# Linear attention and a two-layer MLP in one kernel: the whole hand-written order of steps is replaced

## The chip, the cores and the metric

The kernel runs on one core of a Trainium2 chip. The metric is the device time of one execution in microseconds (us); lower is better. TensorE (PE) multiplies matrices, VectorE (DVE), ScalarE (ACT) and GpSimd (POOL) do elementwise work, SyncE (SP) issues most transfers. Each engine takes its instructions strictly in the order in which the program lists them.

## The reference

A linear attention with a decayed state, for 4 batches, 8 heads, 768 positions and head size 48, whose output goes through a two-layer MLP with a smooth ReLU:

```python
for t in range(S):                       # r, k, v: (B, H, S, D) = (4, 8, 768, 48); w, u: (H, D)
    cur = einsum('bhd,bhe->bhde', u[None] * kt, vt)
    y[:, :, t] = einsum('bhd,bhde->bhe', rt, state + cur)
    state = w[None, :, :, None] * state + einsum('bhd,bhe->bhde', kt, vt)
x = y.transpose(0, 2, 1, 3).reshape(3072, 384)
h = x @ w_in                             # 384 x 2048
g = where(h >= 1, h, where(h <= -1, 0, (h + 1) ** 2 / 4))
out = g @ w_out                          # 2048 x 384
```

## The kernel before

**Tiling.** The 768 positions are cut into 6 chunks of 128, and the 4 batches into 2 pairs. A *group* g (0 to 11) is one chunk of one pair: g // 2 is the chunk, g % 2 the pair. A *unit* n (0 to 23) is one batch of a group: n = 2g + j. Groups 0 and 1 are the first chunk of the two pairs.

**Attention steps of a unit or group.** `load.K`, `load.R`, `loadV` fetch K, R and V (float32, runs of 48 numbers; in groups 0 and 1 in halves by unit, `load.K.0.1` being the second half of group 0). `Ks` and `Rs` scale K and R by powers of the decay (tables made by `Wdn_p`, `Wup_p`, `Wdn`, `Wup` from `bcw`'s product `wb`); `KU` is K times u (`bcu`, `u_bc`), `RKU` is R times KU, `usum` sums it over a head into `diag`, `V` casts V to bfloat16, `V2` is V times diag (a tile that the listings print as `V_` with a number). `T` transposes Ks and Rs on PE for groups 0 to 2 and `TT` copies them out; from group 3 on `KRT` does it by a DMA transpose. `A` multiplies K by R; `AT` masks it into bfloat16, either on DVE in one instruction, or by an ACT copy (`AT.n.1`) and a POOL select (`AT.n.0`). `Sp` multiplies Ks by V, `Tm` adds it to the state (in groups 0 and 1 it writes the first state), `decay` scales the state, `sbf` casts it. `Y` multiplies AT by V and R by the state; `y` adds V2. `X` and `xT` turn y for the MLP: through PE for groups 0 to 2, by one DMA transpose on SP for groups from 3 on (tile `yy`, step `xT.8` for group 4).

**MLP steps.** `mm1.g.q.j` multiplies w_in's quarter q (512 of 2048 columns) by group g's xT into two PSUM banks `h0` to `h2` (j = -1: both units; 0 or 1: one unit, in group 0's first two quarters); `relu` and `square` on ACT and `gate` on DVE apply the smooth ReLU; `mm2.g.j.q` adds quarter q's share to unit j's output; `o` copies it out of PSUM and `out` stores it. Weights are fetched by POOL with a cast to bfloat16: `w_in.0` and `w_in.1` bring quarters 0, 1 and 2, 3; `w_out.q` brings quarter q:

```python
    def w_in_go(e, bk, i):
        n = slice(i * DF // W_IN, (i + 1) * DF // W_IN)
        nc.gpsimd.dma_start(out=w_in_sb[:, :, n], in_=w_in_src[:, :, n])
    def w_out_go(e, bk, i):
        n = slice(i * nF // W_OUT, (i + 1) * nF // W_OUT)
        nc.gpsimd.dma_start(out=w_out_sb[:, n, :], in_=w_out_src[:, n, :])
```

**What sets the order.** A text table, `ORDER`, names every step once; a loop at the end of the kernel runs them in that order, so the table fixes the order on every engine. In a token such as `V.1.0@A:1`, `@A` names the engine (A, D or P), the digits behind the colon the buffers or PSUM banks, and `~5` puts five *idle products* (products of zeros) ahead of the step on PE; `warm.18` is 18 idle products by themselves. Waits follow from the data and the buffers.

```python
    for token in ORDER.split():
        token, _, idles = token.partition("~")
        idle[0] = int(idles or 0)
        name, _, bufs = token.partition(":")
        name, _, e = name.partition("@")
        kind, *args = name.split(".")
        if kind == "warm":
            keep_warm(int(args[0]), *args[1:])
        elif kind in do:
            do[kind](e, [int(x, 36) for x in bufs], *[int(x) if x.lstrip("-").isdigit() else x for x in args])
```

Lines that the profile names: L526 `mm1`, L554 `mm2`, L544 `gate`, L534 `relu`, L539 `square`, L406 `A`, L421, L412 and L416 `AT`, L446 and L441 `Y`, L432 `Sp`, L388 `T`, L501 `X`, L327 `Ks` and `Rs`, L337 `KU`, L344 `RKU`, L355 and L357 `usum`, L369 and L367 `V2`, L468 `y`, L476 and L484 `Tm`, L489 `decay`, L290 `w_in`, L294 `w_out`, L304 the loads, L398 `KRT`, L511 `xT` by DMA, L587 `out`, L204 and L608 idle products, L237 `bcw`, L242 `bcu`, L257 the tables, L232 `lw`. L212 is the helper that copies and casts, for `V`, `TT`, `sbf`, `xT`, `o` and `u_bc`.

Of the kernel before, what the change touches and what calls it, by code (L numbers as in the profile page):

```python
# [14 lines left out]
P = 128  # L15
# [25 lines left out]
usum.1.0@A:1 A.1:0~8 V2.0.0@P:0 Ks.2.0@P:2 AT.2.0:1 loadV.2.0:0 V2.1.0@A:1 Y.0:1 T.3:2 sbf.0@A Tm.2@D usum.0.1@D Y.2:0
TT.3@D:3 y.2:0 AT.1.1:2 Rs.2.0@P:2 A.3:1~14 X.2:0 V2.0.1@A y.0:1 AT.3.0:3 warm.2.h.2 X.0:1 T.5:2~8 AT.1.0 xT.2@A:0
T.4:0 TT.5@D:0 Y.1:0 w_in.1 load.K.3.0:0 xT.0@A:1 sbf.1@A usum.1.1@D A.5:1 mm1.0.0.0:2 KU.2.0@P:0 y.1:2 TT.4@D:1
load.R.3.0:0 V.1.1@A X.1:1 Y.3:0 AT.5.0:0 A.4:0 V2.1.1@P xT.1@A mm1.0.0.1 V.2.0@A:2 Sp.5:1 y.3:0 RKU.2.0@P:0
relu.0.0:0 X.3:0 Tm.5@D:0 mm1.0.1.0:1 AT.4.0:1 xT.3@A decay.5 square.0.0:0 usum.2.0@D:0 Sp.4:1 mm1.0.1.1 w_out.0 Y.4:0
relu.0.1:1 mm1.1.1.-1:0 gate.0.0:0 square.0.1:1 Tm.4@D:1 mm1.0.2.-1:2 relu.1.1:0 Y.5:1 square.1.1:0 V2.2.0@P:0 w_out.1
y.4:1 gate.0.1:1 w_out.2 X.4:0 w_out.3 mm1.0.3.-1:1 xT.4@A:2 gate.1.1:2 relu.0.2:1 Sp.3:0 y.5:2 mm1.1.0.-1:0
square.0.2:1 Tm.3@D KU.3.0@P:1 decay.4 gate.0.2:3 relu.0.3:0 relu.1.0:1 mm2.0.0.0:1 mm2.0.1.0:0 Ks.3.0@P:0
square.1.0:0 KRT.K.3:0 mm1.1.3.-1:2 mm2.0.1.1 Rs.3.0@P:0 RKU.3.0@P:1 mm2.0.0.1 square.0.3:1 gate.1.0:4 mm2.0.1.2 gate.0.3:5
relu.1.3:1 loadV.3.0:1 mm2.0.0.2 mm1.1.2.-1:0 square.1.3:0 usum.3.0@D:1 mm2.0.0.3 relu.1.2:0 KRT.R.3:0 mm2.0.1.3  # L50
o.0.0@D:0 square.1.2:1 mm2.1.0.0:1 o.0.1@D gate.1.3:6 load.K.4.0:1 X.5:0 mm2.1.0.1 load.R.4.0:1 xT.5@A V.3.0@A:3
mm1.2.3.-1:1 gate.1.2:7 sbf.3@A V2.3.0@P:1 Sp.7:0 A.7:2 loadV.4.0:0 relu.2.3:1 Tm.7@D:0 A.6:0 mm2.1.0.2 AT.6.0:2
sbf.2@A square.2.3:0 Ks.4.0@P:2 sbf.4@A Sp.6:0 mm2.1.0.3 load.K.5.0:2 Tm.6@D:1 mm1.2.0.-1:0 o.1.0@A:1 AT.7.0:3 decay.6
Y.6:0 Y.7:1 relu.2.0:0 KRT.K.4:1 y.6:0 mm1.2.1.-1:2 KU.4.0@P:0 y.7 V.4.0@A:4 gate.2.3:8 xT.6:1 RKU.4.0@P:0
square.2.0:1 mm2.1.1.0:0 Sp.8:1 mm2.1.1.1 load.R.5.0:2 Tm.8@D:1 relu.2.1:1 load.K.6.0:0 mm1.2.2.-1:1 gate.2.0:9
Ks.5.0@P:1 mm2.1.1.2 square.2.1:0 mm2.2.0.0:1 mm2.1.1.3 decay.7 Rs.4.0@P:1 mm1.3.0.-1:0 gate.2.1:0 relu.2.2:0
square.2.2:1 KRT.K.5:0 mm2.2.0.1 o.1.1@D sbf.5@A relu.3.0:1 mm1.3.1.-1:2 gate.2.2:1 out.1 KU.5.0@P:1 square.3.0:0
Rs.5.0@P:2 mm2.2.0.2 relu.3.1:0 gate.3.0:3 mm1.3.2.-1:1 KRT.R.4:1 square.3.1:1 loadV.5.0:1 load.R.6.0:0 usum.4.0@D:0
mm2.2.0.3 mm2.2.1.0:0 KU.6.0@P:0 relu.3.2:1 gate.3.1:5 mm1.3.3.-1:0 square.3.2:0 loadV.6.0:0 gate.3.2:4 mm2.2.1.1
V2.4.0@P:0 sbf.6@A o.2.0@A:1 A.9:2 sbf.7@A relu.3.3:0 A.8:1 AT.9.0:1 mm2.2.1.2 KRT.R.5:0 square.3.3:1 mm2.3.0.0:1  # L60
AT.8.0:0 out.0 decay.8 mm2.2.1.3 load.K.7.0:1 mm2.3.0.1 o.2.1@A gate.3.3:2 V.6.0@A:0 V.5.0@A:2 Y.8:0 Ks.6.0@P:0
mm2.3.0.2 y.8:1 Y.9:0 mm2.3.0.3 y.9 RKU.5.0@P:1 A.11:2 xT.8:0 o.3.0@A:0 A.10:1 usum.5.0@D:1 AT.11.0:2 mm2.3.1.0:0
Sp.10:1 KRT.K.6:1 mm2.3.1.1 Rs.6.0@P:0 RKU.6.0@P:0 Tm.10@D:0 mm2.3.1.2 load.R.7.0:1 Sp.9:1 mm2.3.1.3 Tm.9@D:1
V2.5.0@P:1 mm1.4.0.-1:0 AT.10.0:3 o.3.1@A sbf.8@A decay.9 decay.10 KRT.R.6:1 usum.6.0@D:0 relu.4.0:1 Sp.11:1 Y.10:0
mm1.4.1.-1:2 square.4.0:0 Tm.11@D:1 y.10:0 V2.6.0@P:0 Ks.7.0@P:2 Y.11:1 mm1.4.2.-1:1 loadV.7.0:0 out.2 relu.4.1:0
gate.4.0:7 y.11 A.12:0 xT.10:2 square.4.1:1 AT.12.0:0 mm2.4.0.0:0 Sp.12:1 relu.4.2:1 KU.7.0@P:1 square.4.2:0
gate.4.1:6 load.K.8.0:2 mm1.4.3.-1:0 V.7.0@A:1 KRT.K.7:0 gate.4.2:9 load.R.8.0:2 A.13:2 Rs.7.0@P:1 mm2.4.0.1 out.3
# [582 lines left out]
```

## Time and profile before

| what | us |
|---|---|
| median of 3 runs | 175.96 |
| the 3 runs | 175.46, 175.96, 178.86 |
| span of the profiled execution, first to last instruction | 176.4 |
| PE, ACT, DVE, POOL busy | 165.0, 135.2, 130.3, 120.2 |
| matmuls of the first layer (L526) / second layer (L554) | 72.0 / 71.9 |
| first product with w_in starts at | 22.05 |
| last elementwise instruction (L602) starts at | 172.93 |

No time but the span is kept of the profiled execution; the three runs are others. The page lists the busy time of each engine, the span in 40 slices of 4.4 us, the DMA queues, the chain of work that ended last and the costliest groups of instructions. In a row of the timeline the first number is the start, the second the length, then engine, line, operation, output<-inputs, and in brackets how long the engine was idle before and what released it. "DMA to landing" is the time from a transfer's issue to the arrival of its data.

### The profile page before, as it was taken

To read this page: it belongs to the slowest core of one execution; us is meant where nothing else is said; L and a number is where in the kernel's file an instruction comes from. 1 tells how busy PE (TensorE), PEld (TensorE's weight loads), DVE (VectorE), ACT (ScalarE), POOL (GpSimd) and SP (SyncE) were. 2 spreads that over 40 slices of the span, in tenths; PEclk is the share of its full clock that TensorE was granted. 3 is DMA by queue.
4 is the path that set the end of the run, shared out by engine and by line. 5 is a ranking of instruction groups with operands and counts; after the bars stand their busy time and mean duration, and the time that the engine had idled before them with its cause. 6 is when DMAs were issued, how large, how long until landed. Compare 5 with 4: busy or idle time off the path is not lost.

```text
span 176.4 us, 4159 instructions
## 1 busy us (share of the span) xinstructions
PE 165.0 (94%) x1684; PEld 125.2 (71%) x1684; DVE 130.3 (74%) x167; ACT 135.2 (77%) x194; POOL 120.2 (68%) x97
## 2 busy tenths in 40 slices
PE   6998699999999999779999999999999999999992
PEld 5776587766787766458686777885878767777671
DVE  5599779857987578727978889788895877461471
ACT  4399879996987995319989697989399994888540
POOL 6699999990899999999399799999349400000000
PEclk9999999999999999969999999999999999999998
DMA  5999999999999999996999997989982400312022
GB/s 109 221 219 192 216 175 234 207 165 209 238 172 196 191 202 252 158 183 175 196 221 211 185 183 159 266 149 243 194 197 93 89 17 4 97 37 89 4 89 89
DMA packets 106967, 28.78 MB, mean 163 GB/s; under 512 B 100930, under 2 KB 106180, under 8 KB 106948
## 3 DMA queue, kind: packets, MB, share of 16 engines
q1 hardware_dynamic: 103888, 25.24, 73.6%
q0 software_dynamic: 2912, 3.15, 11.4%
q8 instruction: 13, 0.21, 0.5%
q10 hardware_dynamic: 148, 0.13, 0.2%
q14 instruction: 6, 0.05, 0.1%
HBM read 20.45 MB, written 4.72 MB: 143 GB/s over the span
## 4 chain that ended last, share of the span: by engine, by line
PE 71%; DMA 13%; DVE 7%; ACT 5%; POOL 1%; issue 1%; DVEq 0%; POOLq 0%
PE hp L526 31%; PE op L554 30%; DMA VF<-in_v_dram 5%; DMA w_out_sb<-in_moe_w_out_dram 4%; DMA xT<-yy 3%; DVE AT L421 3%; PE A L406 2%; PE Y L446 2%; PE Y L441 2%; PE Sp L432 1%; ACT V L212 1%; PE ub L242 1%; POOL V L369 1%; PE wb L237 1%; ACT RKU L355 1%; DVE yy L468 1%
## 5 line engine op out<-in xcount | busy, mean ns | idle before, releaser
L526 PE MATMUL hp<-xT,w_in_sb 128*128 128x256 bf16 (+1 forms) x600 | 72.0, 271 | 3.4 <-DMA xT<-yy 2.2
L554 PE MATMUL op<-w_out_sb,gt 128*128 128x384 bf16 (+2 forms) x400 | 71.9, 320 | 0.1
L544 DVE SCALAR_TENSOR_TENSOR gt<-sq,hp 128x1024 bf16<-128x1024 f32 x48 | 57.9, 1216 | 16.2 <-ACT sq L539 16.1
L526 PEld LDWEIGHTS <-w_in_sb 128*128 128x128 bf16 x600 | 56.2, 99 | 13.9 <-issue 3.1
L534 ACT ACTIVATE pt<-hp 128x1024 f32<-128x1024 f32 x48 | 48.7, 1018 | 17.7 <-PE hp L526 17.4
L539 ACT ACTIVATE sq<-pt 128x1024 f32<-128x1024 f32 x48 | 50.4, 1057 | 1.2
L554 PEld LDWEIGHTS <-gt 128*128 128x128 bf16 x400 | 36.5, 98 | 19.3 <-issue 0.5
L421 DVE TENSOR_TENSOR AT<-A,umask 128x1024 bf16<-128x1024 f32 x22 | 26.5, 1218 | 2.2 <-PE A L406 1.9
L337 POOL TENSOR_TENSOR KU<-K,u_bc 128x768 f32<-128x768 f32 (+1 forms) x13 | 21.6, 1658 | 2.0 <-DVE u_bc L212 2.0
L344 POOL TENSOR_TENSOR RKU<-R,KU 128x768 f32<-128x768 f32 (+1 forms) x14 | 22.2, 1589 | 0.3
L489 POOL TENSOR_TENSOR state<-Tm,wCm 128x384 f32<-128x384 f32 x16 | 16.0, 1003 | 8.8 <-DVE Tm L476 8.6
L369 POOL TENSOR_TENSOR V<-V,diag 128x768 f32<-128x768 bf16 (+1 forms) x12 | 16.4, 1365 | 7.1 <-ACT V L212 4.7
L327 POOL TENSOR_TENSOR Ks<-Wdn,K 128x768 bf16<-128x768 f32 x10 | 18.2, 1818 | 1.2 <-DMA K<-in_k_dram 1.2
L327 POOL TENSOR_TENSOR Rs<-Wup,R 128x768 bf16<-128x768 f32 x10 | 18.2, 1819 | 0.1
L476 DVE TENSOR_TENSOR Tm<-Sp,state 128x384 f32<-128x384 f32 x16 | 8.9, 555 | 7.3 <-POOL Ks L327 3.4
L468 DVE TENSOR_TENSOR yy<-Y,V 128x384 bf16<-128x384 f32 x18 | 9.9, 554 | 5.0 <-PE Y L446 3.5
L212 ACT CAST V<-VF 128x768 bf16<-128x768 f32 (+1 forms) x14 | 10.2, 737 | 3.6 <-DMA VF<-in_v_dram 3.5
L446 PE MATMUL Y<-V,AT 128*128 128x48 bf16 x192 | 11.4, 185 | 1.2 <-POOL AT L416 0.9
L446 PEld LDWEIGHTS <-AT 128*128 128x128 bf16 x192 | 9.8, 98 | 2.8 <-POOL AT L416 1.3
L357 DVE TENSOR_REDUCE diag<-RKU 128x16 f32<-128x768 f32 (+1 forms) x13 | 11.1, 852 | 0.9 <-POOL RKU L344 0.9
L212 ACT COPY oo<-op 128x384 f32<-128x384 f32 x13 | 6.2, 476 | 6.7 <-PE op L554 6.3
L212 ACT CAST state_bf<-state 128x384 bf16<-128x384 f32 x20 | 10.0, 503 | 0.0
(77 smaller groups left out, 127.2 us busy)
## 6 DMA issues: line engine op xcount, KB each, us to landing
out_dram<-oo SPq DMA_DIRECT2D x11, 384.0 KB, 3.7
K<-in_k_dram SPq DMA_DIRECT2D x10, 384.0 KB, 4.8
R<-in_r_dram SPq DMA_DIRECT2D x10, 384.0 KB, 4.9
VF<-in_v_dram SPq DMA_DIRECT2D x10, 384.0 KB, 5.8
w_in_sb<-in_moe_w_in_dram POOLq DMA_DIRECT2D x2, 768.0 KB, 8.6
w_out_sb<-in_moe_w_out_dram POOLq DMA_DIRECT2D x4, 384.0 KB, 7.5
K<-in_k_dram SPq DMA_DIRECT2D x4, 192.0 KB, 3.8
R<-in_r_dram SPq DMA_DIRECT2D x4, 192.0 KB, 3.7
```

The lines of the kernel that those rows point to most:

```text
L212: nc.scalar.copy(out, in_) if e == "A" else engines[e].tensor_copy(out, in_)
L327: engines[e].tensor_mul(of_unit(dst, j0, j1)[:, :, :, :D], rep(tab, j1 - j0), of_unit(tiles[what, g], j0, j1))
L337: engines[e].tensor_mul(of_unit(tiles["KU", g], j0, j1), of_unit(tiles["K", g], j0, j1), rep(u_bc, j1 - j0))
L344: engines[e].tensor_mul(of_unit(tiles["RKU", g], j0, j1), of_unit(tiles["R", g], j0, j1), of_unit(tiles["KU", g], j0, j1))
L369: engines[e].tensor_mul(tiles["V2", g][:, hs, :], tiles["V", g][:, hs, :], tiles["diag", g][:, hs].unsqueeze(2).to_broadcast([P, hs.stop - ...
L421: nc.vector.tensor_mul(t.rearrange("p i n t -> p (i n) t"), tiles.pop(("A", n)).rearrange("p i n t -> p (i n) t"), umask.unsqueeze(1).to_b ...
L446: nc.tensor.matmul(t[:, 2 * p + i, :], tiles["AT", n][:, i, p, :], tiles["V", g][:, j * H + 2 * p + i, :], start=(c == 0), stop=True, skip ...
L526: nc.tensor.matmul(hp[:, f, cols], w_in_sb[:, i, n0 : n0 + P], tiles["xT", g][:, units, i, :], start=(i == 0), stop=(i == nK - 1), skip_gr ...
L534: nc.scalar.activation(tiles["pt", g, q], tiles["hp", g, q], AF.Relu, bias=0.5, scale=0.5)
L539: nc.scalar.activation(tiles["sq", g, q], tiles.pop(("pt", g, q)), AF.Square, bias=0.0)
L544: nc.vector.scalar_tensor_tensor(out=gt, in0=tiles.pop(("sq", g, q)), scalar=1.0, in1=tiles.pop(("hp", g, q)), op0=ALU.min, op1=ALU.max)
L554: nc.tensor.matmul(t, tiles["gt", g, q][:, f, j * P : (j + 1) * P], w_out_sb[:, n, cols], start=(n == 0), stop=(n == nF - 1),)
```

## The change

Only the table is replaced; no function changes. Every step of before that computes something is still there, on another place and in some cases on another engine or buffer. Its first lines, before and after:

```diff
-warm.18 load.K.0.0:0 load.R.0.0:0 load.K.0.1 load.R.0.1 load.K.1.0:1 load.R.1.0:1 bcu:0 u_bc@D KU.0.0@P:0 RKU.0.0@P:0
+load.R.1.0:2 load.K.1.0:1 lw bcw:0 bcu:1 load.K.0.0:0 load.R.0.0:0 loadV.1.0:0 Wdn_p:2 load.R.0.1 loadV.0.0:1 Wup_p
```

The 18 idle products at the start are gone (62 idle products in all become 44), the product for the decay (`bcw`) comes before that for u (`bcu`), and `u_bc` moves from DVE to ACT.

On POOL's queue, from the first weight transfer on, before (rows in the order of the queue; `w_in_sb` and `w_out_sb` are the weights' tiles, `V_` with a number is V2):

```order
L290 DMA w_in_sb<-in_moe_w_in_dram 128x3x1024
L416 AFFINE_SELECT AT<-AT 128x1024
L369 TENSOR_TENSOR V_327<-V,diag 128x384
L327 TENSOR_TENSOR Ks<-Wdn,K 128x16x48
L327 TENSOR_TENSOR Rs<-Wup,R 128x16x48
L416 AFFINE_SELECT AT<-AT 128x1024
L290 DMA w_in_sb<-in_moe_w_in_dram 128x3x1024
L337 TENSOR_TENSOR KU<-K,u_bc 128x768
L369 TENSOR_TENSOR V_334<-V,diag 128x384
L344 TENSOR_TENSOR RKU<-R,KU 128x768
L489 TENSOR_TENSOR state<-Tm,wCm 128x384
L294 DMA w_out_sb<-in_moe_w_out_dram 128x4x384
```

The same place after the change:

```order
L290 DMA w_in_sb<-in_moe_w_in_dram 128x3x1024
L327 TENSOR_TENSOR Ks<-Wdn,K 128x16x48
L290 DMA w_in_sb<-in_moe_w_in_dram 128x3x1024
L294 DMA w_out_sb<-in_moe_w_out_dram 128x4x384
L416 AFFINE_SELECT AT<-AT 128x1024
L294 DMA w_out_sb<-in_moe_w_out_dram 128x4x384
L369 TENSOR_TENSOR V_313<-V,diag 128x384
L344 TENSOR_TENSOR RKU<-R,KU 128x768
L294 DMA w_out_sb<-in_moe_w_out_dram 128x4x384
L369 TENSOR_TENSOR V_558<-V,diag 128x768
L294 DMA w_out_sb<-in_moe_w_out_dram 128x4x384
```

Between the two w_in transfers stand five steps before and one after; the first select (AT.0.0) and the first V2, which came behind `w_in.0`, now come ahead of it, and w_out's four transfers come earlier among POOL's steps.

On SP's queue, the loads from the tenth to the eighteenth place, before (`VF` is V as loaded, and the number tells tiles apart):

```order
L304 DMA VF_166<-in_v_dram 128x8x48
L304 DMA R_156<-in_r_dram 128x8x48
L304 DMA VF_189<-in_v_dram 128x8x48
L304 DMA K_206<-in_k_dram 128x16x48
L304 DMA R_253<-in_r_dram 128x16x48
L304 DMA VF_189<-in_v_dram 128x8x48
L304 DMA VF_332<-in_v_dram 128x16x48
L304 DMA K_467<-in_k_dram 128x16x48
L304 DMA R_501<-in_r_dram 128x16x48
```

The same places after the change:

```order
L304 DMA R_129<-in_r_dram 128x8x48
L304 DMA VF_147<-in_v_dram 128x8x48
L304 DMA K_131<-in_k_dram 128x8x48
L304 DMA VF_142<-in_v_dram 128x8x48
L304 DMA K_273<-in_k_dram 128x16x48
L304 DMA R_311<-in_r_dram 128x16x48
L304 DMA VF_372<-in_v_dram 128x16x48
L304 DMA R_461<-in_r_dram 128x16x48
L304 DMA K_474<-in_k_dram 128x16x48
```

All twelve halves of groups 0 and 1 (8x48) now come before the first whole group (16x48, group 2), and K of group 2 shares its buffer with group 0, so that its load waits until group 0's K is used.

On DVE, behind the first copy of a transpose (TT.0), which stands on ACT before; here after the change:

```order
L212 CAST V<-VF 128x384
L327 TENSOR_TENSOR Rs<-tab,R 128x8x48
L327 TENSOR_TENSOR Ks<-tab,K 128x8x48
L212 CAST V<-VF 128x384
L337 TENSOR_TENSOR KU<-K,u_bc 128x384
L327 TENSOR_TENSOR Ks<-tab,K 128x8x48
L484 TENSOR_TENSOR state<-Sp,wCm 128x384
L357 TENSOR_REDUCE diag<-RKU 128x8
L327 TENSOR_TENSOR Rs<-tab,R 128x8x48
L484 TENSOR_TENSOR state<-Sp,wCm 128x384
L421 TENSOR_TENSOR AT<-A,umask 128x1024
L344 TENSOR_TENSOR RKU<-R,KU 128x384
```

Two casts of V and an RKU step have moved to DVE here, and later KU.2, Rs.2, RKU.0.1, sbf.0, xT.2 and V2.0.1 as well; TT.1 to TT.5 have left it for ACT, and in all DVE has 14 rows more, POOL 7 fewer.

In the middle of the table, around the first product of group 4, where the DMA transpose `xT.8` is awaited, the step `mm2.3.1.3` changes sides: before the table has `... y.9 ... A.11:2 xT.8:0 ... A.10:1 ... mm2.3.1.0:0 Sp.10:1 ... mm2.3.1.3 ... mm1.4.0.-1:0`, after it `... y.9 ... A.10:0 A.11:1 mm2.3.1.0:1 xT.8:2 ... mm1.4.0.-1:2 mm2.3.1.3`. On PE, `mm1.0.0.0`, the first product with w_in, stands behind `X.1` and `X.3` after the change and ahead of `X.1`, `Y.3`, `A.4` and `X.3` before it.

More of the change, by code (lines that the diff above doesn't have):

```diff
@@ L41 @@
[L41 to L55, printed above, removed]
@@ new lines @@
+Ks.0.0@D:0 load.K.0.1 Rs.1.0@D:2 load.R.1.1 Wup Wdn Rs.0.0@D:1 T.0:0 TT.0@D:3 u_bc@A KU.1.0@P:0 V.1.0@D:3 RKU.1.0@P:1
+loadV.0.1 load.K.1.1 wcol:1 wCm A.0:0~2 Rs.0.1@D KU.0.0@P:1 Ks.1.0@D:2 AT.0.1:3 RKU.0.0@P:0 T.2:1~3 Sp.2:1 KU.1.1@P
+TT.2@A:2 usum.0.0@A:1 V.0.0@D:4 A.2:0~2 KU.0.1@D Ks.0.1@D loadV.1.1 Tm.2@D V.0.1@A AT.0.0 usum.1.0@D:0 Sp.0:0 Rs.1.1@D
+Tm.0@D AT.2.0:0 T.1:1 RKU.1.1@D load.K.2.0:0 Sp.1:1~4 TT.1@A:3 Ks.1.1@D T.3:2 KU.2.0@D:0 Y.2:0~2 Tm.1@D usum.1.1@D
+load.R.2.0:1 V2.1.0@P:1 y.2:1 w_in.0 A.1:0 Y.0:1 Rs.2.0@D:1 V2.0.0@A:0 AT.1.1:0 TT.3@A:3 Ks.2.0@P:0 warm.4.h.1 T.4:1
@@ L100 @@
+mm1.11.3.-1:2 gate.11.2:7 relu.11.3:1 mm2.10.1.2 o.10.0@D:0 mm2.10.1.3 mm2.11.0.0:0 square.11.3:0 mm2.11.0.1 o.10.1@D
+mm2.11.0.2 mm2.11.1.0:1 gate.11.3:4 out.10 mm2.11.0.3 mm2.11.1.1 mm2.11.1.2 o.11.0@A:0 rest.11.0:0 mm2.11.1.3
+rest.11.1 rest.11.2 rest.11.3 out.11.0 ends.11:12
 """
```

103 lines of the change are left out of this document (55 added, 48 removed).

## The prediction

> **What bounds the kernel now.** I read the page first, its busy shares and its 40 slices:
>
> ```profile
> span 176.4 us, 4159 instructions
> ...
> PE 165.0 (94%) x1684; PEld 125.2 (71%) x1684; DVE 130.3 (74%) x167; ACT 135.2 (77%) x194; POOL 120.2 (68%) x97
> ...
> PEclk9999999999999999969999999999999999999998
> DMA  5999999999999999996999997989982400312022
> ```
>
> TensorE is busy 94% of the span, and the 16 DMA engines are full from the second slice to about the 30th. So an order can win only where PE waits: at the start, and around the slice with clock 6. The busy time by stretches shows the second place:
>
> ```profile
> 74.00:76.00 2.00, 0.00 (x0) 0.00 (x0) 1.82 (x2) 0.81 (x2) 1.96 (x3) 1.00 0.10 18
> 76.00:80.00 4.00, 3.94 (x33) 3.15 (x33) 0.79 (x2) 1.15 (x2) 4.00 (x3) 0.57 1.08 212
> ```
>
> After the length come PE, PEld, DVE, ACT, POOL busy, clock, DMA share, GB/s. From 74 to 76 PE does nothing while the DMA engines, too, nearly stand still (share 0.10); behind it the granted clock is 0.57. PE's own rows say what it waited for:
>
> ```profile
> 22.05 0.84 PE L526 MATMUL hp<-xT,w_in_sb 128*128 128x128 bf16 x12 [0.48 <-DMA w_in_sb<-in_moe_w_in_dram]
> 29.18 1.48 PE L526 MATMUL hp<-xT,w_in_sb 128*128 128x256 bf16 x12 [0.29 <-DMA w_in_sb<-in_moe_w_in_dram]
> 36.67 3.01 PE L554 MATMUL op<-w_out_sb,gt 128*128 128x384 bf16 x16
> 76.06 2.72 PE L526 MATMUL hp<-xT,w_in_sb 128*128 128x256 bf16 x12 [2.18 <-DMA xT<-yy]
> ```
>
> The first w_in product starts at 22.05; from there PE is the bound. The chain that ended last gives PE's prices and the three transfers it hangs on:
>
> ```profile
> 13.33 1.13 ACT RKU L355 x10
> 14.46 9.60 DMA VF<-in_v_dram
> 24.08 0.84 ACT V L212
> ...
> 30.26 7.92 DMA w_out_sb<-in_moe_w_out_dram
> 38.22 1.46 PE op L554 x8
> ...
> 45.47 0.55 PE A L406 x16
> ...
> 47.60 1.31 PE hp L526 x12
> ...
> 50.97 0.65 PE op L554 x4
> ...
> 69.31 0.56 DVE yy L468
> 69.89 6.13 DMA xT<-yy
> ```
>
> **The change part by part.** The sum is made against the span, 176.4, which is 0.4 over the median of the runs, 175.96.
>
> *The start.* These rows price it:
>
> ```profile
> 2.94 0.52 ACT L232 ACTIVATE lw_row<-w_row 1x384 f32<-1x384 f32 x1
> 3.55 1.62 PE L242 MATMUL ub<-u_row,ones 97*128 97x384 f32 x2 [0.40 <-DVE wCm L179]
> 6.49 0.56 ACT L257 ACTIVATE tab<-wb,dn_col 128x384 f32<-128x384 f32 x1 [3.04 <-PE wb L237]
> 8.87 0.61 PE L388 MATMUL T<-ident,Rs 128*128 128x128 bf16 x4
> 9.20 1.01 DVE L327 TENSOR_TENSOR Rs<-tab,R 128x384 bf16<-128x384 f32 x2
> 11.52 0.68 DVE L212 COPY TT<-T 128x1024 bf16<-128x1024 bf16 x1
> 14.11 1.21 DVE L421 TENSOR_TENSOR AT<-A,umask 128x1024 bf16<-128x1024 f32 x1
> 15.70 0.54 DVE L357 TENSOR_REDUCE diag<-RKU 128x8 f32<-128x384 f32 x1
> ```
>
> The product for w now goes first: lw ends at 3.46, wb takes 1.6, two tables 1.1, three 384-wide scalings on DVE 1.5, the second half of T.0 0.6 (for the first product that of u, 1.62, is the nearest row), so T.0 is done near 8.4, half a microsecond sooner. But the first w_in product now stands on PE behind X.3, which waits for y.3, and ahead of y.3 DVE has much more than before: TT.0 0.6; nine 384-wide products 4.5 (two take 1.01); two 768-wide (KU.2, Rs.2) 2.0; three first states 1.5; three sums 1.4; four y 2.0 (384-wide too); two AT 2.3; two casts of V, one state cast and one xT, which this trace does not show on DVE: 1.0 at least and 2.9 at most (from a quarter microsecond each to the 0.68 of the wider TT copy), of which I take 1.9, near the 0.5 that ACT takes. Together 16.2, with some 0.4 of waits: y.3 ends at 25.0, X.3 follows, and the first w_in product starts at **25.4, 3.35 later** (2.4 to 4.4 by these bounds). All of that counts, for PE is the bound behind it. PE has then done Y.3, A.4, X.1 and X.3 already (0.8), but 11 idle products (0.6) lie ahead: -0.2.
>
> *The weights.* On POOL:
>
> ```profile
> 8.24 1.00 POOL L337 TENSOR_TENSOR KU<-K,u_bc 128x384 f32<-128x384 f32 x1
> ...
> 13.26 0.93 POOL L290 DMA_DIRECT2D w_in_sb<-in_moe_w_in_dram x1
> 14.20 1.11 POOL L416 TENSOR_SCALAR_AFFINE_SELECT AT<-AT 128x1024 bf16<-128x1024 bf16 x1
> 15.26 0.84 POOL L369 TENSOR_TENSOR V<-V,diag 128x384 f32<-128x384 bf16 x1
> 16.05 1.82 POOL L327 TENSOR_TENSOR Ks<-Wdn,K 128x768 bf16<-128x768 f32 x1
> 20.76 0.80 POOL L290 DMA_DIRECT2D w_in_sb<-in_moe_w_in_dram x1
> ...
> w_in_sb<-in_moe_w_in_dram POOLq DMA_DIRECT2D x2, 768.0 KB, 8.6
> ```
>
> KU.1.1 now waits for the 11th load of SP's list. Before, the load in that place was issued at 9.1 and landed in 3.7 (rows below), at 12.8. Then KU 1.0, AT 1.1, V2 0.84: w_in.0 is issued at 15.8, 2.5 later. Ks.2 follows, and w_in.1 at 18.5 is 2.2 earlier than 20.76; w_out.0 and w_out.1 come right behind. w_out.3 is queued behind V2.2, which waits on DVE's sum of group 2 until about 28: issued near 29.6, it has ten microseconds until mm2.0.0.3, 14.5 of PE work behind 25.4; the last w_out of before took 7.9. With 8.6 to landing w_in.0 is there at 24.4, a microsecond before its product. The w_in.1 and w_out waits of before (0.29, and 38.22 on the chain) should go: from 22.05 to 36.67 PE did 12.8 of work (seven w_in groups 9.2, two w_out 1.3, the small ones 2.3) in 14.6, so 1.8 was lost. SP's R.3 and K.3 now start some 4 later and behind the weights, near 40 by this; their transposes feed A.6, 20.9 of PE work behind 25.4, at 46.3, so I cost them at nothing; without that room each microsecond would count.
>
> What takes their place is V of group 2. Loads wait behind weights:
>
> ```profile
> L304 SPq DMA_DIRECT2D K<-in_k_dram x1: 5325/5325/5325, 17.1 to 17.1; - x1
> DMA to landing us min/median/max: 13.7/13.7/13.7
> ...
> L304 SPq DMA_DIRECT2D VF<-in_v_dram x2: 681/732/782, 7.4 to 9.1; - x2
> DMA to landing us min/median/max: 3.7/3.7/3.7
> ...
> xT<-yy SPq DMA_TRANSPOSE x9, 2.8
> ```
>
> The K load issued at 17.1, under w_in, took 13.7; the V halves, issued before any weights, 3.7. (The last line is for the transposes further down.) V.2's load now needs V.0.1 cast by ACT (behind AT.0 and TT.2 at 1.0 each and 1.8 of sums, ten of whose 16 instructions took 1.13, from A.0's end at 10.9): about 15.2, just ahead of w_in.0, with K.2 and R.2 still in the queue. PE's Sp.5 wants it cast at 27.4, three half groups of 0.67 behind 25.4. The wait is nothing if the load gets through first, and 5 to 6 if it stays behind both w_in halves, for now no gap lies between them. I take 0.8, near the 9.6 that it took before: 15.2 + 9.6 + the cast's 0.84 is 25.6, with 2.5 more for the missing gap. So 1.8 goes, 0.8 comes: **-1.0**.
>
> The Trainium skill, "DMA: Bandwidth & Descriptors", Queues, rings and completion order, has each DMA engine take turns between queues, packet by packet. By that, V.2 would never stand still, the 0.8 would be nothing and the sum lower by as much; the 13.7 beside 3.7 speaks against a share of half.
>
> *The wait at 74.* xT.8 landed after 6.13, and before PE resumed it had lost 2.18 of waiting; then twelve products took 2.72 where 1.31 is usual, and the next small ones lost 0.3: 3.9 in all. In the new order mm2.3.1.3 (0.65) stands behind mm1.4.0 and no longer covers this transfer; some 3.5 of PE work is left between Y.9 and mm1.4.0. The other xT land in 2.7 to 2.8; with 0.6 for yy and about 0.9 in the queue that is 4.3, a wait of 0.8. The bounds: none, or the same slow landing with 0.65 less cover, 2.8 and the clock's 1.75, so 4.6. I take 1.0, by the eight ordinary landings against the one slow one: **-2.9**.
>
> The Trainium skill, "TensorE: Matmul & The Clock Gate", Why this matters for your kernels, wants no idle gap over about 3 us; here a wait of 2.18 brought the clock to 0.57, so the row decides, and by the page even a 2.8 wait would cost no clock.
>
> *The 18 idle products fewer* stand at the very start, where PE waits for ACT anyway: T.0 at 0.61 for four is the price with them. Nothing. The many PE steps from 18 to 25 should bring the clock up in time; if not, 1.7 (half of the 3.4 that the slow stretch lasted: 0.57 over 4 us). The end issues the same stores: nothing.
>
> Sum: 176.4 + 3.35 - 0.2 - 1.0 - 2.9 = 175.65, less 0.4: **175.2**.
>
> **The rivals.** *Starved V (slower).* If over half of V.2's load is left when w_in.0's packets begin, it stays behind both halves: Sp.5 moves from 27.4 to about 32.8, +5.4, and the wait halves the clock as at 76, +1.7, instead of 0.8: 181.5. For it: 13.7 for K; against: V.2 itself took 9.6 with weights in flight.
> *DMA-bound at xT.8 (no change).* Counted in both orders, the same 43 transfers stand ahead of xT.8, and the engines were full nearly all the way. If it lands at 76.0 again, the start is worth nothing: only 0.65 more work is left behind it, 176.4 + 0.65 - 0.4 = 176.7. Against: the standstill from 74 to 76 is no load of work.
> *All waits gone.* No wait for V and none at mm1.4.0, y.3 a microsecond sooner: 175.2 - 0.8 - 1.0 - 1.0 = 172.4; with the start at its lower bound and the early loads helping, 171.9.
>
> **How the numbers follow.** Forecast 0.45, DMA-bound 0.15, starved V 0.23, all waits gone 0.17. A measurement of this kernel tells 2% (3.5 us) from no change. The forecast's own range is 173 to 179; with starved V and the good case in part, **172.0 to 181.5**. Faster (under 172.4) 0.14, slower (over 179.5) 0.25, same 0.61.
>
> **What would show it.** The first w_in product at 25.4 with X.3 just ahead, released by DVE; w_in.0 landed a little before; no wait for w_out near 34 to 40; Sp.5's wait on ACT's V small; the wait at mm1.4.0 near 1 with the clock at full. It is wrong if Sp.5 or mm1.4.0 waits over 3 us, or if DVE reaches y.3 over a microsecond off 25.0.

## The result and the profile after

The changed order takes **184.19 us** (median; 182.87 to 185.79) against 176.01 before on the same chip: ratio 1.046, interval 1.039 to 1.054. It is 4.6% slower, above the upper end of the range. An execution more than 1.5% above the fastest of its kernel is left out of the ratios given here, and of the traces below only that of `start_less_dve` is of such an execution. The profiled execution took 182.87 with a span of 181.2. The lines of its page that answer to those of before:

```profile
span 181.2 us, 4150 instructions
...
PE 165.0 (91%) x1666; PEld 125.4 (69%) x1666; DVE 146.1 (81%) x180; ACT 137.5 (76%) x214; POOL 108.8 (60%) x88
...
PE   2887699999999779999999988999999999999993
...
DVE  5499999995999999798998976889986796565540
...
DMA  5999999996499999869999999997917832040222
```

PE's work is the same 165.0; DVE has 15.8 more (130.3 before) and stands at 9 from the third slice to the sixteenth, but for the tenth; PE's holes lie in the same stretch (fourth and fifth, fourteenth and fifteenth slice). The DMA engines thin out in slices 10 and 11 and move nothing from 44 to 47 us. PE's timeline shows the first w_in product and the longer waits behind it:

```profile
28.53 0.51 PE L501 MATMUL X<-ident,y 128*128 128x128 bf16 x6 [0.25 <-DVE y L468]
28.87 1.34 PE L526 MATMUL hp<-xT,w_in_sb 128*128 128x128 bf16 x21
...
61.30 1.47 PE L526 MATMUL hp<-xT,w_in_sb 128*128 128x256 bf16 x12 [1.34 <-DVE gt L544]
67.88 1.46 PE L554 MATMUL op<-w_out_sb,gt 128*128 128x384 bf16 x8 [1.02 <-DVE Tm L476]
...
109.40 0.62 PE L406 MATMUL A<-RT,KT 48*128 48x128 bf16 x16 [1.50 <-DMA KT<-Ks]
```

The first product starts 6.8 later than before (22.05) and 3.5 later than predicted (25.4). No row of PE waits for w_in, w_out, V or xT. In the chain of work that ended last, everything from TT.0 at 8.54 to the last `y` ahead of X.3 (27.45) stands on DVE. DVE's timeline ahead of the first product, with POOL's beside it (a part of each):

```profile
9.15 0.98 DVE L212 CAST V<-VF 128x384 bf16<-128x384 f32 x1
...
10.98 0.35 DVE L212 CAST V<-VF 128x384 bf16<-128x384 f32 x1
11.25 1.35 DVE L337 TENSOR_TENSOR KU<-K,u_bc 128x384 f32<-128x384 f32 x1
...
17.09 2.72 DVE L337 TENSOR_TENSOR KU<-K,u_bc 128x768 f32<-128x768 f32 x1
...
24.09 1.39 DVE L212 CAST state_bf<-state 128x384 bf16<-128x384 f32 x1
```

```profile
17.17 1.82 POOL L327 TENSOR_TENSOR Ks<-Wdn,K 128x768 bf16<-128x768 f32 x1
...
23.12 2.14 POOL L344 TENSOR_TENSOR RKU<-R,KU 128x768 f32<-128x768 f32 x1
...
37.74 1.82 POOL L327 TENSOR_TENSOR Rs<-Wup,R 128x768 bf16<-128x768 f32 x1 [2.73 <-DMA R<-in_r_dram]
...
41.51 1.81 POOL L337 TENSOR_TENSOR KU<-K,u_bc 128x768 f32<-128x768 f32 x1 [0.87 <-DMA K<-in_k_dram]
```

The same cast takes 0.98 and 0.35; KU of group 2, 2.72. The long ones touch only SBUF and fall on a POOL instruction (KU of group 2 on POOL's Ks at 17.17, the cast of the state on RKU at 23.12). And R of group 3 arrived so late that POOL waited 2.73 for it, and another 0.87 for K: R's load, issued at 23.67, took 14.0 to land, and K's, issued at 24.09, was there near 41.5, when KU starts. On SP's queue the transposes of group 3 then hold up the next load, that of R of group 5 (the last row), since KT waits for Ks, which DVE does at 45.11:

```profile
39.59 2.46 SPq L398 DMA_TRANSPOSE RT<-Rs  x1
46.09 1.23 SPq L398 DMA_TRANSPOSE KT<-Ks  x1
47.42 0.53 SPq L304 DMA_DIRECT2D R<-in_r_dram  x1
```

The view of the loads' line from 23 to 31 us has two landings, R's (14.0) and that of V of group 3 (13.3); K's is not among them:

```profile
DMA to landing us min/median/max: 13.3/13.6/14.0
```

So there were two suspects at the start (DVE held by POOL; the weights ahead of the loads), and the rest of the order as a third. The rivals to them were TensorE's cold start, the changed PE order and SP's blocked queue.

### The profile page after: what moved, and what is told of

The parts are those of the page before. It is cut to its first block, busy times and chain, and to the rows that moved or that the text cites. A ratio compares the mean times of both kernels' runs of the same rounds, so it can differ in the third digit from the quotient of the medians.

```text
span 181.2 us, 4150 instructions
## 1 busy us (share of the span) xinstructions
PE 165.0 (91%) x1666; PEld 125.4 (69%) x1666; DVE 146.1 (81%) x180; ACT 137.5 (76%) x214; POOL 108.8 (60%) x88
## 4 chain that ended last, share of the span: by engine, by line
PE 47%; DVE 18%; POOL 10%; DMA 9%; issue 6%; ACT 5%; SPq 3%; DVEq 0%; POOLq 0%; ACTq 0%
PE op L554 22%; PE hp L526 19%; DVE gt L544 4%; DMA R<-in_r_dram 4%; DMA K<-in_k_dram 3%; POOL Rs L327 3%; DMA KT<-Ks 3%; POOL RKU L344 3%; DVE Rs L327 2%; DVE state_bf L212 2%; ACT sq L539 2%; DVE KU L337 2%; PE A L406 1%; POOL state L489 1%; DVE AT L421 1%
## 5 line engine op out<-in xcount | busy, mean ns | idle before, releaser
L526 PE MATMUL hp<-xT,w_in_sb 128*128 128x256 bf16 (+1 forms) x600 | 69.8, 268 | 2.3 <-DVE gt L544 1.5
L554 PE MATMUL op<-w_out_sb,gt 128*128 128x384 bf16 (+2 forms) x400 | 69.4, 320 | 1.0 <-DVE Tm L476 1.0
L337 POOL TENSOR_TENSOR KU<-K,u_bc 128x768 f32<-128x768 f32 (+1 forms) x12 | 19.6, 1633 | 8.9 <-DMA K<-in_k_dram 4.9
L369 POOL TENSOR_TENSOR V<-V,diag 128x768 f32<-128x768 bf16 (+1 forms) x11 | 15.0, 1361 | 15.2 <-DVE diag L357 15.2
L344 POOL TENSOR_TENSOR RKU<-R,KU 128x768 f32<-128x768 f32 (+1 forms) x11 | 19.5, 1776 | 0.5
L327 POOL TENSOR_TENSOR Rs<-Wup,R 128x768 bf16<-128x768 f32 x8 | 14.6, 1823 | 5.1 <-DMA R<-in_r_dram 5.0
L327 POOL TENSOR_TENSOR Ks<-Wdn,K 128x768 bf16<-128x768 f32 x8 | 14.9, 1859 | 0.1
L212 ACT COPY oo<-op 128x384 f32<-128x384 f32 x17 | 8.1, 474 | 5.0 <-PE op L554 4.5
L357 DVE TENSOR_REDUCE diag<-RKU 128x16 f32<-128x768 f32 (+1 forms) x12 | 10.1, 843 | 0.0
L441 PE MATMUL Y<-state_bf,RT 128*128 128x96 bf16 x72 | 8.6, 204 | 0.0
L212 ACT CAST V<-VF 128x768 bf16<-128x768 f32 (+1 forms) x10 | 7.7, 768 | 1.0 <-DMA VF<-in_v_dram 1.0
```

Source lines behind the costliest of these rows:

```text
L212: nc.scalar.copy(out, in_) if e == "A" else engines[e].tensor_copy(out, in_)
L327: engines[e].tensor_mul(of_unit(dst, j0, j1)[:, :, :, :D], rep(tab, j1 - j0), of_unit(tiles[what, g], j0, j1))
L337: engines[e].tensor_mul(of_unit(tiles["KU", g], j0, j1), of_unit(tiles["K", g], j0, j1), rep(u_bc, j1 - j0))
L344: engines[e].tensor_mul(of_unit(tiles["RKU", g], j0, j1), of_unit(tiles["R", g], j0, j1), of_unit(tiles["KU", g], j0, j1))
L526: nc.tensor.matmul(hp[:, f, cols], w_in_sb[:, i, n0 : n0 + P], tiles["xT", g][:, units, i, :], start=(i == 0), stop=(i == nK - 1), skip_gr ...
L554: nc.tensor.matmul(t, tiles["gt", g, q][:, f, j * P : (j + 1) * P], w_out_sb[:, n, cols], start=(n == 0), stop=(n == nF - 1),)
```

## The experiments

All but the first are tables in the loop's form; a diff names the tokens that differ. Before took 174.5 to 174.7 (median) on the four chips of these runs, and each ratio is to before on the same chip.

### What an SBUF-only DVE instruction costs beside POOL

`port_prices`: no step of the kernel, but seven kinds of DVE instruction, alone and beside POOL's products.

```diff
+for name, op in ops:             # f32, wide, cast, red, psum, pcopy, bf16
+    4 x op()                      # DVE alone
+    4 x nc.gpsimd.tensor_mul(pc, pa, pb)   # 128x768, beside:
+    8 x op()                      # (wide: 5)
```

> This leaves the whole computation out (the output is zeros): seven kinds of DVE instruction, each four times alone and then eight times (the wide one five times) while POOL does four 768-wide products. Theory (a DVE instruction whose operands all lie in SBUF gets no further while POOL works in SBUF): alone 0.35 to 0.55 for 384 wide and 1.0 for 768 wide; beside POOL 1.3 to 1.9 each, ending where a POOL product (1.8) ends; the two kinds that read PSUM the same beside POOL as alone. Rival (both engines just share the memory's bandwidth): every kind grows by the same small share, the PSUM kinds too, and none past 1.3 times. Rival (the long times in the changed kernel were waits that the profile books as work): nothing grows.

Its timeline, for four of the kinds, with three of the four alone in a row and then the eight beside POOL; for the first kind POOL's four stand below, and the last row is POOL's four alone:

```profile
6.31 1.74 DVE L83 TENSOR_TENSOR dc<-da,db 128x384 f32<-128x384 f32 x3
8.09 10.63 DVE L83 TENSOR_TENSOR dc<-da,db 128x384 f32<-128x384 f32 x8
8.16 8.37 POOL L97 TENSOR_TENSOR pc<-pa,pb 128x768 f32<-128x768 f32 x4 [6.69 <-DVE pa L95]
...
33.78 1.15 DVE L85 CAST d<-da 128x384 bf16<-128x384 f32 x3
34.97 9.04 DVE L85 CAST d<-da 128x384 bf16<-128x384 f32 x8
...
44.52 1.73 DVE L86 TENSOR_REDUCE diag<-da 128x8 f32<-128x384 f32 x3
46.28 4.67 DVE L86 TENSOR_REDUCE diag<-da 128x8 f32<-128x384 f32 x8
...
54.13 1.74 DVE L87 TENSOR_TENSOR d<-psa,db 128x384 bf16<-128x384 f32 x3
55.91 4.70 DVE L87 TENSOR_TENSOR d<-psa,db 128x384 bf16<-128x384 f32 x8
...
83.50 7.08 POOL L102 TENSOR_TENSOR pc<-pa,pb 128x768 f32<-128x768 f32 x4 [1.50 <-DVE pa L100]
```

A product of two SBUF tiles takes 0.58 alone. Beside POOL the eight need 10.63; of these some four fall behind POOL's end (16.53 to 18.72, at 0.56), so the four beside POOL's four took 8.4, **2.1 each**: one DVE instruction for each POOL instruction, which itself goes from 1.77 to 2.09. The cast goes from 0.38 to about 1.9 in the same way, and the 768-wide product (not shown) from 0.98 to 2.5. With one operand in PSUM (0.58 and 0.59), and for the reduction from SBUF (0.58 and 0.58), nothing changes. So the theory holds, but for one kind: an SBUF-only reduction is not held. The rule for it stands in the Trainium skill, "SBUF — State Buffer", Who interferes with whom: DVE instructions with two SBUF inputs, and copies and casts in DVE's fast modes, share a pair of ports with POOL, and whoever issues first keeps it for the whole instruction; a reduction never does. All these kinds agree, and so does one DVE instruction to one of POOL; that the first to issue wins is shown by no run here.

### Start and rest exchanged

`b_start_a_rest` and `a_start_b_rest`: one order up to xT.3, where both have done nearly the same steps, then the other.

```diff
-ORDER = before                    # or after
+ORDER = (before up to xT.3) + (the steps of after that are not yet there)
+ORDER = (after up to xT.3) + (the steps of before that are not yet there)
```

> Order of before up to xT.3 (118 steps), then the order of the change. Theory (the loss lies in the start, the first w_in product at 28.9 instead of 22.05, and the rest of the new order is some 2 us better since xT.8 no longer waits): 174, first product at 22. Rival (the loss lies behind the start too: DVE and SP queues that stand at 56 to 61 and at 43 to 47): 179 or more.

> Order of the change up to xT.3 (119 steps), then the order of before. Theory (loss in the start): first product at 28.9, 181 to 183. Rival (loss behind the start): 177.

Measured 182.35 (ratio 1.045, 1.042 to 1.049) and 182.36 (1.036, 1.028 to 1.045; its profiled execution 179.75). Neither theory alone: by the ratios the new rest costs 7.9 and the new start, with its weights close together, 6.3, where both together cost 8.2. With before's start the first product is at 22.22, but w_out.0 to 2 go out together at 25.9, R of group 3 lands so late that POOL waits 10.1 us for it, and PE waits for w_out at 38.6 (1.81) and at 50.2 (2.01, for a gate).

### The start with before's engines

`a_order_b_engines`: 20 steps of the change's start back on the engine of before.

```diff
-V.1.0@D V.0.0@D RKU.1.1@D KU.2.0@D Rs.2.0@D RKU.0.1@D sbf.0@D V2.0.1@D TT.1@A ...
+V.1.0@A V.0.0@A RKU.1.1@P KU.2.0@P Rs.2.0@P RKU.0.1@P sbf.0@A V2.0.1@A TT.1@D ...
```

> Order of the change, but the 20 steps of the start that it gave to another engine are back on the engine of before (casts of V, sums, casts of the state, KU, RKU and Rs of the start). Theory (SBUF-only work on DVE beside POOL made the start long): first product near 25, 179. Rival (the order itself, group 1 ahead of group 0 and the weights close together, made it long): first product at 28 or later, 182 to 184.

Measured 185.91 (1.066, 1.062 to 1.070): a miss, the first product at 32.6. T of group 2 waited 4.31 for POOL's Ks: KU.2 and Rs.2 now stand ahead of it on POOL, which needs 1.8 for each where DVE alone needs 0.95, and this order leaves it no time. It does not tell the theories apart, since it moved work to an engine that then became the bound.

### Two steps out of DVE's way; the idle products back; the middle; the weights by themselves

```diff
 start_less_dve (from after)
-KU.2.0@D ahead of Y.2, sbf.0@D
+KU.2.0@D ahead of RKU.2.0@P (behind y.3), sbf.0@A
 idle_back (from after)
+warm.18 at the start
 middle_less_dve (from after)
-sbf.3@D sbf.7@D sbf.6@D sbf.4@D V2.4.0@D
+sbf.3@A sbf.7@A sbf.6@A sbf.4@A V2.4.0@P
 weights_alone (from before)
-w_in.0 ... Ks.2.0@P ... Rs.2.0@P ... w_in.1 ... w_out.0 ... w_out.1
+w_in.0 ... Ks.2.0@P w_in.1 w_out.0 w_out.1 ... Rs.2.0@P
```

> The change, with two SBUF-only steps out of DVE's way to the first w_in product: KU.2 stays on DVE but behind y.3, the cast of state 0 goes to ACT. Theory (they were held there by POOL: 2.72 and 1.39 where 0.98 and 0.35 is their price alone): first product 4.1 sooner, near 24.8 to 25.5, total 179. Rival (they cost only their own work, 1.3): first product at 27.5, total 181.5. Rival (PE's cold clock or the order of groups sets the start): first product at 28.5 or later.

> The change, with the 18 idle products back at the very start. Theory (DVE sets the start, PE's speed there does not): first product at 28.4 to 28.9, total within 0.5 of the change, though the transposes of T take 0.40 instead of 0.61 from 12 on. Rival (the cold TensorE made the start long): T's transposes short and the first product 1.5 or more sooner, total 181.

> The change, with five SBUF-only steps of its middle (casts of states 3, 4, 6, 7 and V2 of group 4) back on ACT and POOL as before. Theory (DVE, held by POOL, is the bound from 45 to 72): the waits of PE on DVE at 51, 61 and 68 (2.6 together) go, total 180 to 181. Rival (ACT and POOL are as late as DVE was; POOL's queue is the bound): waits of the same size on ACT or POOL, total 183 or more.

> The order of before, with w_in.1, w_out.0 and w_out.1 issued close behind w_in.0 (behind Ks of group 2) and nothing else moved. Theory (weights close together are not what costs: the queues take turns packet by packet, so loads of V, K and R come at half speed but not last): 174.5 to 175.5, the w_in.1 and w_out waits gone. Rival (loads of V.2, K.3, R.3 starve behind the weights): waits of PE on V or of POOL on R and K of 2 or more, total 178 or more.

`start_less_dve`, PE's and ACT's timeline:

```profile
25.80 2.48 PE L522 MATMUL hp<-xT,w_in_sb 128*128 128x128 bf16 x36
...
33.87 0.80 PE L428 MATMUL Sp<-V,Ks 128*128 128x96 bf16 x8 [5.59 <-ACT xT L208]
...
32.61 0.83 ACT L208 CAST V<-VF 128x768 bf16<-128x768 f32 x1 [6.30 <-DMA VF<-in_v_dram]
```

The first product comes 3.1 sooner, more than the 1.3 that the two steps cost by themselves, and near what was forecast (24.8 to 25.5). But the total is hardly better: 181.86 in one execution and 184.94 to 185.41 in three, of which the trace shows that of 185.23. Behind the first products Sp stands 5.59, for V of group 2, whose load has only just landed at 32.6 (the row names xT.3, which follows that cast on ACT and frees Sp's bank). How long the wait was in the execution of 181.86 is not known; two other kernels below show it with 6.1 and 4.0. This is the "starved V" of the prediction. Its load was issued at 15.59 in both kernels, but w_in.0 at 15.97 here and 16.23 there, where V was cast at 29.28 without a wait: DVE's delay covers whatever the load lacked there. (A side effect: RKU of group 2 now waits for KU, and w_out.2 behind it is issued at 28.1 instead of 25.2.)

`weights_alone`: 183.36 (1.052, 1.047 to 1.057). Moving three transfers in the **old** order costs 8.8, as much as the whole change:

```profile
22.05 0.40 PE L384 MATMUL T<-ident,Rs 128*128 128x128 bf16 x4 [2.84 <-POOL Rs L323]
...
33.42 0.48 PE L428 MATMUL Sp<-V,Ks 128*128 128x96 bf16 x4 [6.13 <-ACT V L208]
...
32.54 0.83 ACT L208 CAST V<-VF 128x768 bf16<-128x768 f32 x1 [6.17 <-DMA VF<-in_v_dram]
```

POOL, which issues them at 0.8 each, comes to Rs of group 2 at 20.17 instead of 17.95, and T waits 2.84 for it (0.76 before); then Sp waits 6.1 for V. The rival of this run was right. The load of a later group issued at 15.4 stays 8.9 us at its issue on SP, and one of the loads issued from 13 to 16 took 18.9 to land.

`idle_back`: 186.23 (1.068, 1.065 to 1.072). The idle products shorten nothing: T's transposes stay at 0.61 for four, and the first product comes at 31.3. So this run does not remove the slow TensorE that the rival names; `start_less_dve` speaks against that rival, since its T's take 0.61 too and its first product comes at 25.8. `middle_less_dve`: 184.78 (1.056, 1.051 to 1.061), first product at 29.8. In both, the computing steps of the start are those of the change, yet DVE's rows (of `middle_less_dve` here, POOL's below) differ:

```profile
16.98 0.96 DVE L334 TENSOR_TENSOR KU<-K,u_bc 128x768 f32<-128x768 f32 x1
...
23.40 2.39 DVE L209 CAST state_bf<-state 128x384 bf16<-128x384 f32 x1
...
17.04 2.57 POOL L324 TENSOR_TENSOR Ks<-Wdn,K 128x768 bf16<-128x768 f32 x1
```

Here KU takes 0.96 and POOL's Ks 2.57; in the changed kernel KU took 2.72 and Ks 1.82. In both the two start within 0.1 us of each other, and one of them pays for the other's whole length; the starts in the trace don't show why which. So the start of this order ends between 27 and 31 us from kernel to kernel. In the middle PE's waits for gates and Tm at 61 and 68 (2.4) became 0.8 for xT and 0.4 for a gate; from the first product to the end it takes 151.8 instead of 152.3. With this spread that run settles nothing on the total.

### The weights apart, and each kind alone

```diff
 weights_spread (from after)
-w_in.0 Ks.2.0@P w_in.1 w_out.0 ... w_out.1 ... RKU.2.0@P w_out.2 ... V2.2.0@P w_out.3
+w_in.0 Ks.2.0@P ... w_in.1 RKU.2.0@P w_out.0 ... V2.2.0@P w_out.1 w_out.2 w_out.3
 spread_less_dve: the same, with the two steps of start_less_dve
 w_in_alone (from before):  +w_in.1 close behind w_in.0 (behind Ks.2.0@P)
 w_out_alone (from before): +w_out.0 w_out.1 right behind w_in.1 in its old place
```

> The change, with its weights issued apart as before: w_in.1 ahead of RKU of group 2 (about 23), w_out.0 behind it (26), w_out.1 to 3 behind V2 of group 2 (32); nothing else moved. Theory (two bounds at the start, DVE till 28.5 and the load of V of group 2 behind the weights till 29 to 32; with the weights apart only DVE's is left): first product still at 28.5 to 28.9, but R and K of group 3 land near 30 and not 36 to 41, the SP queue no longer stands from 43 to 46: total 178 to 180. Rival (weights cost nothing in this order, since DVE is later anyway): 182 to 184.

> The same, with KU of group 2 behind y.3 on DVE and the cast of state 0 on ACT as in the second pair of runs. Theory (both bounds gone): first product near 25.5 as there, and no wait of 5 us for V of group 2 at Sp.5: 175.5 to 178. Rival (the weights apart don't help V of group 2, it is late by the loads ahead of it): the 5.6 wait stays, total 181 or more.

> The order of before, with only w_in.1 issued close behind w_in.0. Theory (w_in.1's packets keep the load of V of group 2 from landing): Sp.5 waits for V 4 to 6, total 179 to 181. Rival (the w_out quarters do it): Sp.5's wait under 1, total 174.5 to 175.5.

> The order of before, with only w_out.0 and w_out.1 issued sooner, right behind w_in.1 in its old place (21.6 and 22.4 instead of 26.9 and 29.5). Theory (V of group 2 has landed by then, so nothing that is needed soon stands behind them but K and R of group 3): total 174.5 to 176, a wait of POOL on R or K of group 3 of some us. Rival (the w_out quarters are what starves V): Sp.5 waits 3 or more, total 178 or more.

`weights_spread`: 182.83 (1.043, 1.035 to 1.051), no different from the change; POOL waits for no load of group 3 now, but DVE's start remains (27.0 in the profiled execution, where KU came first), PE waits 1.4 for w_out, and 1.66 and 0.30 for DVE at 61 and 67. `spread_less_dve`: 180.43 (1.033, 1.027 to 1.039):

```profile
25.77 1.50 PE L523 MATMUL hp<-xT,w_in_sb 128*128 128x128 bf16 x24
...
26.18 0.84 ACT L209 CAST V<-VF 128x768 bf16<-128x768 f32 x1
...
40.61 0.81 PE L551 MATMUL op<-w_out_sb,gt 128*128 128x384 bf16 x4 [1.37 <-DMA w_out_sb<-in_moe_w_out_dram]
```

V is cast at 26.18 without a wait, as expected, where with the weights close it was 32.61. Both bounds of the start had to go for one to help; what is left above 178 the theory had missed.

`w_in_alone`: 179.76 (1.030, 1.026 to 1.034). `w_out_alone`: 179.22 (1.029, 1.021 to 1.036), though the theory gave 174.5 to 176:

```profile
29.20 0.48 PE L428 MATMUL Sp<-V,Ks 128*128 128x96 bf16 x4 [4.02 <-ACT V L208]
```

```profile
23.66 0.83 ACT L208 CAST V<-VF 128x768 bf16<-128x768 f32 x1 [0.57 <-DMA VF<-in_v_dram]
...
25.80 0.56 DVE L464 TENSOR_TENSOR y<-Y,V 128x384 bf16<-128x384 f32 x1 [2.12 <-POOL V L365]
...
35.00 1.82 POOL L333 TENSOR_TENSOR KU<-K,u_bc 128x768 f32<-128x768 f32 x1 [3.08 <-DMA K<-in_k_dram]
...
44.60 0.95 DVE L353 TENSOR_REDUCE diag<-RKU 128x16 f32<-128x768 f32 x1 [2.97 <-POOL RKU L340]
```

The first row is `w_in_alone`'s, the others `w_out_alone`'s. w_in.1 keeps V of group 2 away (4.0); the two w_out quarters don't, but they keep K and R of group 3 away (POOL waits 3.1 and 1.4). PE waits 1.5 at 26 and 1.5 at 46, both times for DVE, and for two reasons. At 26 it is POOL's time: its V2 comes at 24.93 instead of 23.36, behind two issues of 0.76 each, and `y` waits 2.12 for it; no load is in that path. At 46 it is the loads: DVE's `usum` of group 3 waits 2.97 for RKU, which stands behind K and R on POOL, and behind `usum` stands the copy of `o` that PE needs. The 5.1 and 4.5 add up to 9.6, a little over the 8.8 of both.

### Start and rest apart, with the weights in their old places

```diff
 b_start_a_rest_spread: b_start_a_rest, with w_out.0 ahead of V2.2.0@P, w_out.1 to 3 behind it
 b_start_a_rest_less:   the same, with
-sbf.3@D sbf.4@D sbf.6@D sbf.7@D V2.4.0@D Rs.4.0@D Ks.3.0@D Ks.5.0@D
+sbf.3@A sbf.4@A sbf.6@A sbf.7@A V2.4.0@P Rs.4.0@P Ks.3.0@P Ks.5.0@P
 a_start_less_b_rest:   spread_less_dve up to xT.3, then before (with before's places of w_out)
 before_no_idle:        before without warm.18
```

> The start and the places of all weights as before, behind xT.3 the order of the change. Theory (the earlier run with this start lost its time to w_out.0 to 2 issued together at 26, which kept R of group 3 away until 41; what is left of the rest's own cost is DVE's queue between 45 and 70): 176.5 to 178, PE waits for gates near 60 stay at 1 to 2, POOL waits for R of group 3 under 3. Rival (the order of the rest is itself slow, SP's queue above all): 180 or more.

> The same, with the eight SBUF-only steps of the middle (casts of states 3, 4, 6, 7, V2 and Rs of group 4, Ks of groups 3 and 5) back on ACT and POOL. Theory (DVE, held by POOL, is what the rest costs): 1 to 2 less than the run beside it, 175 to 176, the waits for gates gone. Rival (ACT and POOL are as full): the same or more, the waits at the same places on other engines.

> The start of the change with KU of group 2 behind y.3, the cast of state 0 on ACT and w_in.1 behind X.3 (about 25 by its queue), then the order of before with its places of w_out. Theory (the start costs its own delay, 25.8 instead of 22.05, less what before loses at xT.8): 176.5 to 178.5. Rival (the start costs nothing once PE is the bound behind it, or the rest of before needs its own start): 175 or less, or 180 or more.

> Before, without the 18 idle products at its very start. Theory (TensorE's speed there hardly matters, other engines set the start): T's transposes at 0.61 for four until past 15 instead of 0.38 to 0.40, the first w_in product within 0.5 of 22.05, total 174.3 to 175.2. Rival (a cold TensorE makes the start long): first product 1 to 2 later, total 176 or more.

`a_start_less_b_rest`: 177.34 (1.015, 1.011 to 1.019), as expected: the new start, mended, costs 2.7. `b_start_a_rest_spread`: 181.23 (1.035, 1.029 to 1.040) and `b_start_a_rest_less`: 180.23 (1.033, 1.027 to 1.038): the rival was right, by the ratio the rest of the new order costs some 6.0 with before's start and weights, and with the eight steps off DVE some 5.7; the difference lies within the intervals. PE's waits in `b_start_a_rest_less`:

```profile
36.78 0.81 PE L550 MATMUL op<-w_out_sb,gt 128*128 128x384 bf16 x4 [0.77 <-DMA w_out_sb<-in_moe_w_out_dram]
39.43 0.81 PE L550 MATMUL op<-w_out_sb,gt 128*128 128x384 bf16 x4 [1.84 <-DMA w_out_sb<-in_moe_w_out_dram]
...
68.89 0.40 PE L402 MATMUL A<-RT,KT 48*128 48x128 bf16 x8 [1.08 <-DVE gt L540]
79.15 1.47 PE L522 MATMUL hp<-xT,w_in_sb 128*128 128x256 bf16 x12 [1.44 <-DMA xT<-yy]
```

The new rest asks for w_out sooner than the old places deliver it (2.9 in all), and for gates and xT.8 sooner than they are done. So the order needs its w_out early, and w_out early keeps the loads away. What part of the 6.0 each wait makes was not measured.

`before_no_idle`: 174.55 (1.000, 0.997 to 1.003). The idle products are worth nothing. Its page and PE's timeline also show the old order in an execution without the stall at xT.8:

```profile
span 172.6 us, 4123 instructions
```

```profile
21.95 0.84 PE L522 MATMUL hp<-xT,w_in_sb 128*128 128x128 bf16 x12 [0.42 <-DMA w_in_sb<-in_moe_w_in_dram]
...
80.56 1.47 PE L522 MATMUL hp<-xT,w_in_sb 128*128 128x256 bf16 x12 [0.39 <-DVE AT L417]
```

From 32 to 78 us PE waits once, 0.34 for w_out; there is no wait for xT.8 and the clock stays at 1.0. No version beat before.

## Why the prediction was wrong, step by step

- **The first w_in product at 25.4** was 28.87. The chain was the right one (X.3 behind y.3, on DVE without a pause), but a term was mis-sized: the two casts of V, the cast of the state and xT, taken at 1.9, took 0.98 + 0.35 + 1.39 + 0.34 = 3.1, above even the upper bound of 2.9, and KU.2 and Rs.2, taken at 2.0, took 2.72 + 1.30 = 4.0. This is the step that failed: I priced SBUF-only steps by rows in which POOL left DVE alone, and so put the wait for POOL at nothing. Four of them lost 0.63, 0.80, 1.77 and 1.04 (the rows above, less 0.35, 0.55, 0.95 and 0.35).
- **The weights, -1.0.** The waits for w_in.1 and w_out did go. The change shows no wait for V, but with its start at 28.9; in the trace with the first product at 25.8, near where I put it, the wait was 5.59 and not 0.8. The rival "starved V" (5 to 6) had the right size and place; its condition, that most of the load is left when w_in's packets begin, fits the issue times of 15.59 and 15.97. "V.2 itself took 9.6 with weights in flight" was weak evidence against it, since that row had a gap of 7.5 us between the two w_in transfers.
- **R.3 and K.3 "cost nothing".** They were there near 37.7 and 41.5, where I had said 40, and POOL stood for them. SP then held RT and KT for POOL and DVE, with the next loads behind, and the DMA engines moved nothing from 44 to 47. But A.6 and A.7 wait for no transpose (the only wait there is 0.24 for a gate), and `weights_spread`, where POOL waits for neither load, is no faster beyond the intervals (PE waits 1.4 for w_out there instead). So for PE the term held as far as the runs show; what the pause of SP's queue cost later is open. In the old order, with less room, such a delay costs the 1.5 at 46 of `w_out_alone`.
- **The wait for xT.8, -2.9.** The changed kernel has no wait there, but neither has the old order in `before_no_idle`. The 176.4 was a span, and an execution takes about 1.7 more than its span (182.87 against 181.2), so that execution took some 178.1, not "0.4 over the median": most of the 3.9 was its own. To subtract it from the median was a second error, of about 2.
- **The 18 idle products: nothing.** Right (1.000).
- **The rest: nothing.** I looked at the start and at xT.8 and let the other steps behind them pass. Beside `before_no_idle` (span 172.6, first product at 21.95) the changed execution is 8.6 longer: 6.9 ahead of the first product and 1.7 behind it (152.3 against 150.6; another chip). Behind the first product the change waits 4.9 (0.18 + 0.24 + 1.34 + 1.02 + 0.40 + 0.26 + 1.50), before_no_idle 1.8 (0.23 + 0.25 + 0.31 + 0.34 + 0.28 + 0.39). The gates before 61 came late behind a state cast on DVE that takes 0.35 alone and 1.97 here, again beside POOL:

```profile
57.02 1.97 DVE L212 CAST state_bf<-state 128x384 bf16<-128x384 f32 x1
58.91 2.34 DVE L544 SCALAR_TENSOR_TENSOR gt<-sq,hp 128x1024 bf16<-128x1024 f32 x2
```

What remains: the shares don't add up (6.3 for the start with its weights and 7.9 for the rest, 2.7 for a mended start, 6.0 for the rest with the old places of the weights, 8.8 for three weights moved in the old order, 8.2 for the whole change). That one delay hides another is shown for V of group 2 and argued for the others. The late start and the starved loads are shown each by runs of their own; within the rest only the waits are shown, not the price of each.

## What to carry to other kernels

Give a DVE product, copy or cast two prices, alone and beside POOL, if all its operands lie in SBUF: before moving such work to DVE, look what POOL does at that time. Before transfers are moved together, list what is queued behind them, on the DMA queues and on the engine that issues them, in the order in which it will be needed. And when a delay is removed, ask what it was hiding: here DVE's late start covered a late load.

## What was not expected of the hardware

POOL and DVE take turns instruction by instruction on SBUF-only work: 2.1 for a DVE product of 0.58, and 2.57 for POOL's Ks of 1.82 where POOL was the one held. The profile books that wait as execution, so DVE looked 81% busy. The clock fell also around waits for data: the granted clock of `weights_alone` was 0.97 over the run, with slices of 0.6, 0.7 and 0.5 from 23 to 36 us, around its waits of 2.84 and 6.13:

```profile
PEclk9999967599999999999999999999999999999999
```

The length of the wait alone does not tell it: behind the 1.54 of `w_out_alone` the clock was 0.57 from 26 to 28 us, and with the 1.84 of `b_start_a_rest_less` no slice is below 9. Nor does the granted clock tell all: it is 1.0 throughout the changed kernel, yet A's eight products take 0.61 there as late as 23.58 and 0.40 only from 27.34 on, where before takes 0.40 for them at 21.18.
